# Attention and a Fourier mix on one core: the copy of attention sums goes to ScalarE, with an own order of products after each half, and the last reciprocal is taken on 16 columns

## The chip, the core and the metric

The kernel runs on one core of a Trainium2 chip. The core has five engines with queues of their own: TensorE (PE, its weight loads PEld), VectorE (DVE), ScalarE (ACT), GpSimd (POOL) and SyncE (SP), which here issues transfers only. TensorE writes into eight PSUM banks of 128 partitions x 512 fp32 values; VectorE and ScalarE read them out into SBUF. The metric is the device time of one execution in microseconds (us), the median of several.

## The reference

The input `x` has 2048 rows of 512. Two mixes of it are blended by a gate of each row:

```python
g = sigmoid((x * gate_w).sum(-1))                    # one number a row
q, k, v = split(x @ wqkv, heads=32, width=16)        # 32 heads
p = softmax((q @ k.T) * 16 ** -0.5)                  # 2048 x 2048 for each head
a = concat_heads(p @ v) @ wo
b = Re(DFT_seq(DFT_hidden(x)))                       # as products with cosines and sines
out = g * a + (1 - g) * b
```

## The kernel before

Heads are worked in 16 pairs (`NP`). A pair has two halves of 1024 queries, and a half has 16 steps, one for each block of 128 keys. Three kinds of product share TensorE; each uses 64 of its 128 rows, and products on the two row groups run side by side (the digit in a token is the row group):

- `e`, a score (line 725): keys x 512 queries into a PSUM bank. ScalarE takes the exponential out of it (line 707).
- `c`, a scan (line 758): scores of a later pair, of which VectorE takes only the maximum (line 760), since the softmax is shifted by it.
- `s`, a spectral product (line 983) of the Fourier part, summed over 48 products in the banks `z0` and `z1` and read out by VectorE (line 890, 892) when a group is complete.

Scores and scans share five banks, `b0` to `b4`. A planner, the class `Banks`, gives each of them the bank that is free soonest by its own model of when the engines get there; its constants (`period`, `release`, `late`) are times in ns. It moves nothing else: the order on TensorE is written out by hand.

From macro step `SINGLES` = 90 to `OUTM` = 234 the work stands in 72 blocks of two macro steps, that is, four steps of a half. The list `BLOCKS` says how many spectral products for each row group a block has: 24 in 48 of the blocks, 16 in 24 of them. `BLOCK_ORDERS` holds the order of the tokens of a block. All blocks of a size use one order. At the end of a block the value products of its four steps follow (`pv`, line 737): `e` times values, summed into one bank `pvb` over the 16 steps of a half. A column of ones beside the values gives the denominators of the softmax, one row of `pvb` in each of four quadrants.

After the 16th step `quotients` copies `pvb` to `ob` (line 770 or 772). GpSimd's queue sends the four denominator rows to a small tile `lc` (line 775); three macro steps later `divide` takes the reciprocal there, sends it to HBM and back, spread over partitions (`rb`), and multiplies on GpSimd (line 790). None of that is on TensorE. The next half's first value products come a block later, and overwrite `pvb`.

Four blocks make a half, so every fourth block follows a half end: 18 of the 72 blocks, 12 of size 24 and 6 of size 16.

The last half can't wait for transfers. Line 1184 copies it out in two halves of 256 columns; a product with a selection matrix `sel` (line 1188, built at the start in line 86) spreads the denominators over 128 partitions, VectorE takes reciprocals of 128 x 256 twice (lines 1200 and 1207) and multiplies, ScalarE and VectorE or GpSimd split the result into a high and a low part (`oh`, `ol`), and the last products of rows 8 to 15 (`part(t, 2)`, line 219) use these. "Row t" here is a block of 128 output rows. VectorE adds each product into its row (line 928), or ScalarE scales it and GpSimd adds (lines 1195 and 1196). The rows are then sent to HBM by SyncE's and ScalarE's queues (line 1220). Ten rows are still to be sent at this point.

Of the kernel before, what the change touches and what calls it, by code (L numbers as in the profile page):

```python
# [18 lines left out]
P = 128  # L19
# [36 lines left out]
}  # L56
BLOCK_SCANS = {24: 8, 16: 4}


def build(tc, x, xT, wqkv, wo, wrT, wiT, cr, ci, gate, out):  # L60
    nc = tc.nc
    with ExitStack() as ctx:
# [21 lines left out]
        sel = keep.tile([P, 4, 32], F32, name="sel")  # L84
        for n in range(4):
            nc.vector.tensor_copy(sel[:, n, :], ident[:, 32 * n + DH:32 * n + VC].to_broadcast([P, 32]))
        sel = sel.rearrange("p n m -> p (n m)")
# [546 lines left out]
        with ExitStack() as pa:  # L634
# [8 lines left out]
            def bank(tag, name="s"):  # L643
                return pools[0].tile([P, 512], F32, tag=tag, name=name)
# [18 lines left out]
            class Banks:  # L663

                slot, late, gap, load, group, weights, second = 226.0, 425.0, 93.0, 207.0, 854.0, 103.0, 56.0
# [101 lines left out]
            def quotients(p, h):  # L767
                ob = ap.tile([P, 512], F32, tag="ob", name="ob", bufs=2)
                if now[0] < OUTM - 1:
                    nc.vector.tensor_copy(ob, pvb)  # L770
                else:
                    nc.scalar.copy(ob, pvb)
                lc = sm.tile([P, 16], F32, tag="lc", name="lc")
                for n, (c, j, r) in enumerate(quads):
                    nc.gpsimd.dma_start(lc[32 * n:32 * n + 32, :],  # L775
                                        ob[r + DH:r + VC, :].rearrange("p (s e) -> p s e", e=16))
                return p, h, ob, lc
# [318 lines left out]
            for m in range(MACROS):  # L1096
# [46 lines left out]
                elif (m - SINGLES) % 2 == 0:  # L1143
                    size = BLOCKS[(m - SINGLES) // 2]
                    whole_block = BLOCK_ORDERS[size].split()
# [40 lines left out]
            spread = [bank("b0", "spread"), bank("b1", "spread")]  # L1186
            for c, ps in zip(halves_, spread):
                nc.tensor.matmul(ps[:, c], sel, ob[:, c], start=True, stop=True)
            part(3, 2)
            part(11, 0, 1)  # L1190

            def scaled(t, j):

                o = ap.tile([P, D], F32, tag="take", name="take", bufs=3)
                nc.scalar.mul(o, groups[t][j], g[:, t + 4 * j:t + 4 * j + 1])
                return lambda: nc.gpsimd.tensor_add(ys[t + 4 * j], ys[t + 4 * j], o)

            add = [scaled(3, j) for j in range(2)]
            c, ps = halves_[0], spread[0]
            nc.vector.reciprocal(rb[:, c], ps[:, c])  # L1200
            nc.vector.tensor_mul(ob[:, c], ob[:, c], rb[:, c])
            nc.scalar.copy(oh[:, c], ob[:, c])
            nc.gpsimd.tensor_sub(ol[:, c], ob[:, c], oh[:, c].bitcast(F32))
            for t in (8, 9):
                part(t, 2)
            c, ps = halves_[1], spread[1]
            nc.vector.reciprocal(rb[:, c], ps[:, c])
            nc.vector.tensor_mul(ob[:, c], ob[:, c], rb[:, c])
            nc.scalar.copy(oh[:, c], ob[:, c])
            nc.vector.tensor_sub(ol[:, c], ob[:, c], oh[:, c].bitcast(F32))  # L1210
            take_in(8, groups[8][0])
            for f in [scaled(8, 1)] + add:
                f()
            for t in (10, 11):
                part(t, 2)
# [31 lines left out]
```

## Time and profile before

| | us |
|---|---|
| median of three runs (1694.23 to 1701.38) | 1694.77 |
| the profiled execution's own time | 1694.55 |
| its span, first to last instruction | 1692.8 |
| first value product | 339.9 |
| value products of the first half end within the blocks, from | 716.95 |
| last value products of all | 1674.5 |

The profile's rows read: engine, line, operation, tile written <- tiles read; partitions x elements; then times. A group row gives the count, the busy time in us and the mean of one in ns, and after the bar the idle time before and what ended it. A row of a timeline starts with the start in us and the duration in us of neighbouring instructions that are merged, with their count behind `x`; in brackets stands the idle time ahead. A row of the chain in order of time has the start, the length and the count. VectorE and ScalarE overlap neighbouring instructions a little, so their starts are closer than their durations. A product of plain fp32 operands (the value products, the turn of the last half) appears as two loads and two products in the trace and as one in the order of instructions.

### The profile page before, as it was taken

To read this page: it belongs to the slowest core of one execution; us is meant where nothing else is said; L and a number is where in the kernel's file an instruction comes from. 1 tells how busy PE (TensorE), PEld (TensorE's weight loads), DVE (VectorE), ACT (ScalarE), POOL (GpSimd) and SP (SyncE) were. 2 spreads that over 40 slices of the span, in tenths; PEclk is the share of its full clock that TensorE was granted. 3 is DMA by queue.
4 is the path that set the end of the run, shared out by engine and by line. 5 is a ranking of instruction groups with operands and counts; after the bars stand their busy time and mean duration, and the time that the engine had idled before them with its cause. 6 is when DMAs were issued, how large, how long until landed. Compare 5 with 4: busy or idle time off the path is not lost.

```text
span 1692.8 us, 37028 instructions
## 1 busy us (share of the span) xinstructions
PE 1677.6 (99%) x13675; PEld 1074.6 (63%) x13675; DVE 1268.8 (75%) x2377; ACT 1291.3 (76%) x2410; POOL 706.6 (42%) x890
## 2 busy tenths in 40 slices
PE   9999999999999999999999999999999999999997
PEld 7877778833333333777776777566777777656554
DVE  5799899777777777888888888556888888656334
ACT  5689988799999999666665566777556665777885
POOL 1464301454662322364454444444535445445321
PEclk9999999999999999999999999999999999999999
DMA  8765234554542222243332332573332423335512
GB/s 281 234 231 154 68 121 145 176 187 126 144 128 70 61 70 74 64 115 95 92 100 82 101 97 86 149 245 87 118 107 80 127 90 113 104 108 151 160 40 100
DMA packets 140549, 206.61 MB, mean 122 GB/s; under 512 B 58880, under 2 KB 61936, under 8 KB 140368
## 3 DMA queue, kind: packets, MB, share of 16 engines
q1 hardware_dynamic: 98096, 173.76, 33.1%
q0 software_dynamic: 41696, 29.44, 6.7%
q8 instruction: 108, 1.77, 0.4%
q10 hardware_dynamic: 576, 1.05, 0.2%
q14 instruction: 73, 0.60, 0.1%
HBM read 137.89 MB, written 65.81 MB: 120 GB/s over the span
## 4 chain that ended last, share of the span: by engine, by line
PE 97%; DVE 1%; ACT 1%; issue 1%; POOL 0%; DVEq 0%; ACTq 0%; POOLq 0%
PE pvb L737 28%; PE z L983 24%; PE s L725 17%; PE s L758 9%; PE xy L350 6%; PE xy L371 6%; PE s L187 5%; PE s L364 0%; DVE y L928 0%; DVE fold L193 0%; DVE el L468 0%; ACT fold L191 0%; ACT eh L467 0%; PE s L611 0%; DVE rb L1200 0%
## 5 line engine op out<-in xcount | busy, mean ns | idle before, releaser
L707 ACT ACTIVATE e<-s 128x512 f32<-128x512 f32 (+1 forms) x1862 | 1014.4, 678 | 318.1 <-PE s L758 247.3
L760 DVE TENSOR_REDUCE mx<-s 128x1 f32<-128x512 f32 x1320 | 869.0, 688 | 233.3 <-PE s L758 167.3
L725 PE MATMUL s<-qs,ks 50*128 50x512 f32 x2040 | 620.1, 418 | 0.1
L983 PE MATMUL z<-b,chi 64*128 64x512 f32 x2060 | 513.9, 392 | 0.0
L737 PE MATMUL pvb<-e,va 128*17 128x512 f32 x4096 | 492.7, 595 | 0.3 <-DVE ob L770 0.3
L725 PEld LDWEIGHTS s<-qs,ks 50*128 50x128 f32 x2040 | 306.6, 185 | 212.0 <-ACT e L707 153.3
L758 PE MATMUL s<-ks,qs 48*128 48x512 f32 x1320 | 427.9, 402 | 0.0
L983 PE MATMUL z<-b,clo 64*128 64x512 f32 x1030 | 337.4, 394 | 0.0
L983 PEld LDWEIGHTS z<-b,chi 64*128 64x128 f32 x2060 | 324.8, 186 | 15.2
L193 DVE CUSTOM_DVE_ANT_0 fold<-s,fold 128x512 f32<-128x512 f32 x364 | 239.9, 689 | 24.6 <-ACT fold L191 7.4
L758 PEld LDWEIGHTS s<-ks,qs 48*128 48x128 f32 x1320 | 226.0, 185 | 34.5 <-issue 18.7
L737 PEld LDWEIGHTS pvb<-e,va 128*17 128x17 f32 x4096 | 92.2, 96 | 242.4 <-issue 237.3
L187 PE MATMUL s<-ks,qs 48*128 48x512 f32 x728 | 232.4, 400 | 1.6 <-ACT fold L191 1.2
L191 ACT ACTIVATE fold<-s 128x512 f32<-128x512 f32 x364 | 201.1, 605 | 28.0 <-PE s L187 26.9
L983 PEld LDWEIGHTS z<-b,clo 64*128 64x128 f32 x1030 | 173.5, 186 | 10.4 <-POOL clo L254 3.1
L775 POOL DMA_DIRECT2D lc<-ob x124 | 62.5, 510 | 249.9 <-DVE ob L770 214.1
L253 POOL CAST chi<-craw 128x512 fp32r<-128x512 f32 x126 | 77.3, 614 | 212.9 <-PE z L983 131.5
L254 POOL TENSOR_TENSOR clo<-craw,chi 128x512 fp32r<-128x512 f32 x126 | 161.8, 1284 | 10.4
L187 PEld LDWEIGHTS s<-ks,qs 48*128 48x128 f32 x728 | 132.6, 184 | 36.5 <-DVE mx L193 12.6
L371 PE MATMUL xy<-w,b 64*128 64x512 f32 x384 | 120.3, 399 | 0.0
L350 PE MATMUL xy<-w,b 64*128 64x512 f32 x384 | 117.0, 393 | 0.0
L928 DVE SCALAR_TENSOR_TENSOR y<-z,g,y 128x512 f32<-128x512 f32 x44 | 32.5, 750 | 75.2 <-PE z L983 69.7
(138 smaller groups left out, 1518.1 us busy)
## 6 DMA issues: line engine op xcount, KB each, us to landing
craw<-cr SPq DMA_DIRECT2D x64, 256.0 KB
craw<-ci SPq DMA_DIRECT2D x64, 256.0 KB
qs<-q_d SPq DMA_DIRECT2D x126, 128.0 KB
ks<-k_d SPq DMA_DIRECT2D x108, 128.0 KB
ab_d<-ab SPq DMA_DIRECT2D x32, 256.0 KB
y_d<-y SPq DMA_DIRECT2D x32, 256.0 KB
b<-bs_d SPq DMA_DIRECT2D x32, 256.0 KB
qs<-q_d SPq DMA_DIRECT2D x126, 64.0 KB
```

The costliest lines, as they stand in the source:

```text
L187: nc.tensor.matmul(ps, rows.q[qb // 8][b:b + 48, qb % 8 * P:(qb % 8 + 1) * P], rows.k[c // 2][b:b + 48, c % 2 * 512:(c % 2 + 1) * 512], st ...
L191: seen_by(nc.scalar.activation(fold[j], ps, AF.Relu))
L193: seen_by(nc.vector.tensor_tensor_reduce(out=fold[j], in0=ps, in1=fold[j], scale=1.0, scalar=-3.0e38, op0=ALU.add, op1=ALU.max, accum_out= ...
L254: sub(lo, raw, hi.bitcast(F32))
L350: ins = nc.tensor.matmul(ps, lhs[64:P], rhs[64:P], start=False, stop=last)
L371: nc.tensor.matmul(ps, lhs[0:64], rhs[0:64], start=n == 0, stop=False)
L707: nc.scalar.activation(e if j is None else e[:, j * 512:j * 512 + 512], ps, AF.Exp, scale=SCALE)
L725: nc.tensor.matmul(ps, rows.k[kb // 8][b:b + 50, kb % 8 * P:(kb % 8 + 1) * P], rows.q[h][b:b + 50, c * 512:c * 512 + 512], start=True, sto ...
L737: nc.tensor.matmul(pvb[r:r + VC, :], va[:, kb, 2 * p + j, :], es[step][c][0][:, j * 512:j * 512 + 512], start=kb == 0, stop=kb == NB - 1, ...
L758: nc.tensor.matmul(ps, rows.q[qb // 8][b:b + 48, qb % 8 * P:(qb % 8 + 1) * P], rows.k[c // 2][b:b + 48, c % 2 * 512:(c % 2 + 1) * 512], st ...
L760: nc.vector.tensor_reduce(mx[p][:, j, qb, c:c + 1], ps, axis=AX.X, op=ALU.max)
L983: nc.tensor.matmul(ps, pr_.lhs(j), pr_.rhs(j), start=group.count[j] == 1, stop=group.count[j] == group.size)
```

## The change

In the 18 half ends within the blocks ScalarE copies `pvb` instead of VectorE, as it did before in the last two; the copy is entered in `Banks` as 872 ns of ScalarE's time. The block behind a half end takes its tokens from a table of its own, `AFTER_HALF`, with the same numbers of `e`, `c` and `s`. In the last half, four products with four columns of the identity turn the denominators onto partitions (`den`, 128 x 16); the reciprocal is taken there, VectorE copies it out to 256 columns for each half of the columns (`inv4`), and four products with the identity turn it back, spread over 32 partitions each, into PSUM, from where VectorE multiplies with it. The two subtractions for `ol` are both on VectorE. GpSimd adds rows 3, 7, 12 and 13 instead of 3, 7 and 12, without being put back behind the turn. The transfers of the rows are dealt out anew, with rows 3 and 7 first.

```diff
+AFTER_HALF = {
...
+    16: "c0 e1 s0 s1 e0 c1 s0 s1 s0 e1 s0 s1 c0 s1 e0 s1 s0 s1 e0 c1 s0 s1 e0 s1 s0 c1 e0 s1 s0 s1 c0 e1 s0 s1 s0 e1 s1 c0 e1 s0 s1 s0 c1 e0 s1 s0 e1 s0 s1 e0 s0 e1 s0 s1 e0 e1",
+}
...
-        sel = keep.tile([P, 4, 32], F32, name="sel")
-        for n in range(4):
-            nc.vector.tensor_copy(sel[:, n, :], ident[:, 32 * n + DH:32 * n + VC].to_broadcast([P, 32]))
-        sel = sel.rearrange("p n m -> p (n m)")
...
-                slot, late, gap, load, group, weights, second = 226.0, 425.0, 93.0, 207.0, 854.0, 103.0, 56.0
+                slot, late, gap, load, group, weights, second, copy = 226.0, 425.0, 93.0, 207.0, 854.0, 103.0, 56.0, 872.0
...
                 ob = ap.tile([P, 512], F32, tag="ob", name="ob", bufs=2)
-                if now[0] < OUTM - 1:
+                if now[0] < SINGLES:
                     nc.vector.tensor_copy(ob, pvb)
                 else:
                     nc.scalar.copy(ob, pvb)
+                    banks.engine["e"] = max(banks.engine["e"], banks.t + banks.copy)
...
-                    whole_block = BLOCK_ORDERS[size].split()
+                    whole_block = (BLOCK_ORDERS if m % (NB // 2) else AFTER_HALF)[size].split()
...
-            spread = [bank("b0", "spread"), bank("b1", "spread")]
-            for c, ps in zip(halves_, spread):
-                nc.tensor.matmul(ps[:, c], sel, ob[:, c], start=True, stop=True)
-            part(3, 2)
-            part(11, 0, 1)
+            den = bank("b3", "den")
+            for b in range(4):
+                nc.tensor.matmul(den[:, 4 * b:4 * b + 4], ob[:, P * b:P * b + P], ident[:, DH:P:32], start=True, stop=True)
+            inv = sm.tile([P, 16], F32, name="inv")
+            nc.vector.reciprocal(inv, den[:, 0:16])
...
-                return lambda: nc.gpsimd.tensor_add(ys[t + 4 * j], ys[t + 4 * j], o)
...
+                nc.gpsimd.tensor_add(ys[t + 4 * j], ys[t + 4 * j], o)
+
+            part(3, 2)
+            for j in range(2):
+                scaled(3, j)
+            wide_ = ap.tile([P, 16, 32], F32, tag="ob", name="inv4", bufs=2)
+            spread = [bank("b0", "spread"), bank("b1", "spread")]
+            for h, c in enumerate(halves_):
+                nc.vector.tensor_copy(wide_[:, 8 * h:8 * h + 8], inv[:, 8 * h:8 * h + 8].to_broadcast([P, 8, 32]))
+                for b in (2 * h, 2 * h + 1):
+                    nc.tensor.matmul(spread[h][:, P * b:P * b + P], wide_[:, 4 * b:4 * b + 4].rearrange("p n k -> p (n k)"),
+                                     ident, start=True, stop=True)
+                part(11, h)
+                nc.vector.tensor_mul(ob[:, c], ob[:, c], spread[h][:, c])
+            for c in halves_:
+                nc.scalar.copy(oh[:, c], ob[:, c])
+                nc.vector.tensor_sub(ol[:, c], ob[:, c], oh[:, c].bitcast(F32))
+            for t in (8, 9, 10, 11):
                 part(t, 2)
-            for t, j in ((9, 0), (9, 1), (10, 0), (10, 1), (11, 0), (11, 1)):
-                take_in(t + 4 * j, groups[t][j])
-            for queue, rows in ((nc.sync, (8, 9, 3, 10, 7, 11)), (nc.scalar, (12, 13, 14, 15))):
+                take_in(t, groups[t][0])
+                if t < 10:
+                    scaled(t, 1)
+                else:
+                    take_in(t + 4, groups[t][1])
+            for queue, rows in ((nc.sync, (3, 7, 8, 12, 13)), (nc.scalar, (9, 10, 14, 11, 15))):
```

TensorE at the first half end within the blocks: the last value products (`pvb`) and what follows, before.

```order
L737 MATMUL pvb<-e,va 17x512 x16
L725 MATMUL s<-qs,ks 128x512
L758 MATMUL s<-ks,qs 128x512
L983 MATMUL z<-b_5729,chi 128x512
L725 MATMUL s<-qs,ks 128x512
L983 MATMUL z<-b_5730,chi 128x512
L983 MATMUL z<-b_5729,chi 128x512
L983 MATMUL z<-b_5729,clo 128x512
L758 MATMUL s<-ks,qs 128x512
L725 MATMUL s<-qs,ks 128x512
```

The same place now:

```order
L737 MATMUL pvb<-e,va 17x512 x16
L725 MATMUL s<-qs,ks 128x512
L758 MATMUL s<-ks,qs 128x512
L725 MATMUL s<-qs,ks 128x512
L758 MATMUL s<-ks,qs 128x512
L984 MATMUL z<-b_5724,chi 128x512
L725 MATMUL s<-qs,ks 128x512
L984 MATMUL z<-b_5725,chi 128x512
L984 MATMUL z<-b_5724,chi 128x512
L984 MATMUL z<-b_5724,clo 128x512
```

A second score and a second scan have moved ahead of the first spectral product (`z`), which gives ScalarE and VectorE two pieces each in the first four products.

ScalarE from the last blocks to its end, before; `e` are exponentials, `take` rows scaled for GpSimd, `chi` high parts.

```order
L707 ACTIVATE e<-s 128x512 x1210
L772 COPY ob<-pvb 128x512
L707 ACTIVATE e<-s 128x512 x64
L772 COPY ob<-pvb 128x512
L707 ACTIVATE e<-s 128x512 x56
L1195 ACTIVATE take<-s_24958,g 128x512
L1195 ACTIVATE take<-s_24959,g 128x512
L1202 CAST chi<-ob 128x256
L1209 CAST chi<-ob 128x256
L1195 ACTIVATE take<-s_25004,g 128x512
```

Now the copies stand among the exponentials; the start of what was one stretch of 1210:

```order
L707 ACTIVATE e<-s 128x512 x50
L772 COPY ob<-pvb 128x512
L707 ACTIVATE e<-s 128x512 x64
L772 COPY ob<-pvb 128x512
L707 ACTIVATE e<-s 128x512 x64
```

Every 64 exponentials, which are one half, a copy of the sums has come in; it is behind all exponentials of the half and ahead of those of the next.

VectorE in the last half, from the copy of the sums to the first row (`y`), before.

```order
L1184 COPY ob<-pvb 128x256 x2
L1200 RECIPROCAL rb<-spread 128x256
L1201 TENSOR_TENSOR ob<-ob,rb 128x256
L1207 RECIPROCAL rb<-spread 128x256
L1208 TENSOR_TENSOR ob<-ob,rb 128x256
L1210 TENSOR_TENSOR clo<-ob,chi 128x256
L928 SCALAR_TENSOR_TENSOR y_23635<-s_25003,g,y_23635 128x512
```

And now:

```order
L1185 COPY ob<-pvb 128x256 x2
L1191 RECIPROCAL inv<-den 128x16
L1205 COPY inv_24986<-inv 128x256
L1210 TENSOR_TENSOR ob<-ob,spread 128x256
L1205 COPY inv_24986<-inv 128x256
L1210 TENSOR_TENSOR ob<-ob,spread 128x256
L1213 TENSOR_TENSOR clo<-ob,chi 128x256 x2
L929 SCALAR_TENSOR_TENSOR y_23630<-s_25014,g,y_23630 128x512
```

One reciprocal of 16 columns stands where two of 256 stood, two copies out to 256 columns have come in, each ahead of products on TensorE that its multiplication waits for, and both subtractions now stand ahead of the first row.

More of the change, by code (lines that the diff above doesn't have):

```diff
@@ L56 @@
 }
+AFTER_HALF = {
+    24: "e0 c1 e0 c1 s0 e1 s0 s1 s0 s1 s1 s0 s1 c0 e1 s0 s1 s0 c1 s0 s1 e0 e1 s0 s1 c0 s1 s0 s1 s0 e0 c1 e0 s1 s0 s1 c0 s1 s0 e1 s1 s0 c1 s0 s1 e0 s1 s0 e1 c0 s1 s0 s0 e1 s0 c1 e0 s1 s0 s1 c0 e1 s0 s1 s0 e1 s0 c1 c0 s1 s0 s1 e0 s1 s0 s1 c0 s1 c0 c1",
+    16: "c0 e1 s0 s1 e0 c1 s0 s1 s0 e1 s0 s1 c0 s1 e0 s1 s0 s1 e0 c1 s0 s1 e0 s1 s0 c1 e0 s1 s0 s1 c0 e1 s0 s1 s0 e1 s1 c0 e1 s0 s1 s0 c1 e0 s1 s0 e1 s0 s1 e0 s0 e1 s0 s1 e0 e1",
+}
 BLOCK_SCANS = {24: 8, 16: 4}
@@ L1195, in scaled @@
                 nc.scalar.mul(o, groups[t][j], g[:, t + 4 * j:t + 4 * j + 1])
[L1196 to L1203, printed above, removed]
@@ L1204, in build @@
-            for t in (8, 9):
-                part(t, 2)
[L1206 to L1215, printed above, removed]
```

## The prediction

> **What bounds the kernel.** I read the page first (busy times, then the chain), next the chain stretch by stretch, next the timelines of VectorE, ScalarE and TensorE at one half end, and last the timeline of the final 20 us.
>
> ```profile
> PE 1677.6 (99%) x13675; PEld 1074.6 (63%) x13675; DVE 1268.8 (75%) x2377; ACT 1291.3 (76%) x2410; POOL 706.6 (42%) x890
> PE 97%; DVE 1%; ACT 1%; issue 1%; POOL 0%; DVEq 0%; ACTq 0%; POOLq 0%
> ```
>
> TensorE sets the time: 97% of the chain is its own. What another engine does counts only where TensorE waits for a PSUM bank, and behind TensorE's last product. The page cannot show such a wait, since a product that starts late still reads as busy. The chain in order of time can: each block of products ends in one run of value products (`pvb`), so the distance of two runs is the length of a block. A half ends in the run at 716.95 (blocks of 24) and in the run at 1509.94 (blocks of 16).
>
> ```profile
> 716.95 3.56 PE pvb L737 x32
> 730.37 3.56 PE pvb L737 x32
> 743.55 3.56 PE pvb L737 x32
> ...
> 1509.94 3.56 PE pvb L737 x32
> 1520.45 3.56 PE pvb L737 x32
> 1530.72 3.56 PE pvb L737 x32
> ```
>
> A block of 24 after a half end lasts 730.37 - 716.95 = 13.42 us, the next one 13.18. A block of 16 after a half end lasts 10.51 us, the next one 10.27. So a half end costs 0.24 us in either kind. There are 72 blocks, four to a half: 18 half ends, 12 before blocks of 24 and 6 before blocks of 16.
>
> **What the 0.24 us are.** The copy of the sums stands ahead of the scans on VectorE:
>
> ```profile
> L770 DVE COPY ob<-pvb x29: 690/692/694, 369.6 to 1555.1; 128x512 f32<-128x512 f32 x29
> ...
> 720.64 0.69 DVE L770 COPY ob<-pvb 128x512 f32<-128x512 f32 x1 [1.73 <-PE pvb L737]
> 721.25 4.69 DVE L760 TENSOR_REDUCE mx<-s 128x1 f32<-128x512 f32 x7
> ...
> 734.42 4.97 DVE L760 TENSOR_REDUCE mx<-s 128x1 f32<-128x512 f32 x7 [0.47 <-PE s L758]
> ...
> 720.44 0.50 PE L725 MATMUL s<-qs,ks 50*128 50x512 f32 x1
> 733.86 0.49 PE L725 MATMUL s<-qs,ks 50*128 50x512 f32 x1
> ```
>
> After a half end the first scan is read 721.25 - 720.44 = 0.81 us after the block's first product; in the next block 734.42 - 733.86 = 0.56. VectorE starts 0.25 us late, reads scans back to back, and TensorE, which has five banks for scores and scans together, loses about the same 0.24 us later in the block.
>
> **Part 1: the copy on ScalarE.** It leaves VectorE at these 18 half ends (the 11 earlier ones of the 29 stay). The last two half ends already do it this way:
>
> ```profile
> L772 ACT COPY ob<-pvb x2: 586/586/587, 1599.3 to 1639.9; 128x512 f32<-128x512 f32 x2
> ...
> 1639.76 0.50 PE L983 MATMUL z<-b,b 64*128 64x512 f32 x1
> ...
> 1639.94 0.59 ACT L772 COPY ob<-pvb 128x512 f32<-128x512 f32 x1 [0.49 <-issue]
> 1640.42 3.13 ACT L707 ACTIVATE e<-s 128x512 f32<-128x512 f32 x6
> ...
> 734.45 6.16 ACT L707 ACTIVATE e<-s 128x512 f32<-128x512 f32 x12 [4.79 <-PE s L758]
> 1524.57 8.01 ACT L707 ACTIVATE e<-s 128x512 f32<-128x512 f32 x16 [2.28 <-PE s L725]
> ```
>
> The copy itself is hidden: ScalarE stands idle for 4.79 us (2.28 in a block of 16) while the value products run, and nothing is queued ahead of the copy. Behind it wait the exponentials of the new block. The first can start 1640.42 - 1639.76 = 0.66 us after the block's first product; without a copy it starts 734.45 - 733.86 = 0.59 us after. So ScalarE is put back by 0.07 us where VectorE was put back by 0.25. If this cover were gone (a copy that starts late), up to 0.59 us would stand before the first exponential, and in a block of 16 ScalarE has no pause to make it up: there 16 exponentials run back to back for 8.01 us of 10.27. The GpSimd DMAs that wait for the copy get their sums 0.1 us sooner and stand on no path.
>
> **Part 2: the own order after a half end.** It has as many products of each kind, so TensorE's own work is the same; only waits can differ. In a block of 24 it feeds two scores and two scans before the first spectral product, where the old one feeds one of each: ScalarE and VectorE both have a second piece of work sooner. No trace shows this order. Bounds: at best no wait is left and a block costs what its neighbours cost, 18 x 0.24 = 4.3 us gained; at the other end one wait as large as the old one stays, 0 gained. Passing on the whole 0.07 us would take back 1.3. I take 0.03 us lost in each, near the good end since 0.07 is the largest delay that a row gives: 18 x (0.24 - 0.03) = 3.8 us gained.
>
> **Part 3: the last half.** From here on the chain leaves TensorE:
>
> ```profile
> 1675.07 1.23 PEld L219 LDWEIGHTS s<-b,b 64*128 64x128 f32 x12 [0.85 <-issue]
> 1675.30 0.76 DVE L1184 COPY ob<-pvb 128x256 f32<-128x256 f32 x2 [2.50 <-PE pvb L737]
> 1676.66 0.73 PEld L1188 LDWEIGHTS spread<-ob,sel 128*128 128x128 f32 x4 [0.36 <-issue]
> 1677.45 1.76 DVE L1200 RECIPROCAL rb<-spread 128x256 f32<-128x256 f32 x1 [1.39 <-issue]
> 1678.72 1.27 ACT L1195 ACTIVATE take<-s,g 128x512 f32<-128x512 f32 x2 [5.67 <-PE s L219]
> 1681.38 0.43 DVE L1208 TENSOR_TENSOR ob<-ob,rb 128x256 f32<-128x256 f32 x1
> 1682.62 4.03 DVE L928 SCALAR_TENSOR_TENSOR y<-s,g,y 128x512 f32<-128x512 f32 x6
> 1682.91 3.73 POOL L1196 TENSOR_TENSOR y<-y,take 128x512 f32<-128x512 f32 x3 [1.81 <-ACT take L1195]
> ...
> L782 DVE RECIPROCAL lc<-lc 128x16 f32<-128x16 f32 x31 | 7.6, 244 | 0.0
> GB/s 0 0 0 312 382 304 0 0 0 31 0 0 0 0 0 0 0 0 0 0 0 0 0 269 379 382 382 375 367 394 390 367 383 382 378 390 156 0 0 0
> ```
>
> The last row cuts 1672 to 1693 into 40 slices of 0.525 us. From the first finished row on the writes run at about 382 GB/s without a hole until 1691: ten rows of 262 KB at 0.69 us are 6.9 us, longer than VectorE's seven remaining sums (to 1687.3). So the end is the first row's time plus the queue of rows. The change touches both.
>
> The queue: rows 3 and 7 no longer wait behind the turn; they leave before row 8. Eight rows remain, 2 x 0.69 = 1.4 us less. Rows 12 and 13 need 0.68 us on ScalarE and 1.27 on GpSimd behind row 8's products, and come before the queue reaches them.
>
> The first row: now VectorE starts row 8 at 1682.62. New steps from 1676.66, when the array is free: 8 passes for `den` (four products, two passes each, as the two of L1188 gave four loads). A load costs between (1.23 - 0.18) / 11 = 0.095 (half-height weights) and, nearest in shape, (0.73 - 0.19) / 3 = 0.18 us; I take 0.18: done at 1678.2 with 0.25 us through the array. Reciprocal of 16 columns 0.24 (two of 1.76 go). Copy out to 256 columns about 0.42: 1678.9. Four passes and the way back to VectorE 0.95: 1679.8. Product 0.43: 1680.2. Then the second half's copy, its passes (0.95), its product (0.43), one subtraction (0.43) and the third product of row 8 (0.3): with nothing in the way row 8 starts at 1682.7, no gain from the shorter reciprocals, because the way over TensorE is walked twice in a row.
>
> But something is in the way. GpSimd now adds row 3 from about 1679.8 on (the passes of `part(3, 2)` follow `den`, ScalarE needs 0.68), and beside a GpSimd operation VectorE's SBUF-to-SBUF work is held:
>
> ```profile
> L211 DVE CAST chi<-mt x16: 172/181/1229, 110.3 to 1563.2; 128x32 fp32r<-128x32 f32 x16
> ...
> 1562.66 1.28 POOL L840 TENSOR_TENSOR b<-wor,b 128x512 fp32r<-128x512 f32 x1
> 1563.21 1.23 DVE L211 CAST chi<-mt 128x32 fp32r<-128x32 f32 x1
> ```
>
> A cast of 0.18 us took 1.23 when it met a GpSimd sum. The second copy of the turn, due at 1680.2, meets row 3's sum (to 1681.1) and waits 0.9 us: row 8 starts at 1683.6, 1.0 later than now. The sums of rows read PSUM and go on beside GpSimd (the 4.03 us beside the 3.73). Together -1.4 + 1.0 = -0.4 us. Ends: no meeting (-1.4 + 0.1) and loads at 0.095 (16 passes, 1.4 sooner), -2.7; both GpSimd sums ahead of the copy, another 1.27, +0.9. I take -0.4.
>
> A rule that would spoil this part: the Trainium skill (FP8 and Floating Point Precision, TensorE Precision Notes) says that a true FP32 product takes four passes through the array. By it the turn has 16 more passes than I counted. The rows show two loads for each call, against it.
>
> **Part 4: the four copies for `sel` go.** They stand before 2.4 us, while TensorE waits for its first loads: nothing.
>
> **Sum.** 1692.8 of span - 3.8 - 0.4 = 1688.6, against a profiled run of 1694.55 with its start and end: 1690.35. The median of the runs shown is 0.22 above that run: 1694.77 - 4.2 = **1690.6 us**.
>
> **Rivals.** *A, the wait only moves.* The new order leaves one wait per block, for a bank of an exponential instead of a scan: blocks gain 0, 1694.4. For it: five banks serve both engines and no row has the order. Against: the delay is 0.07 instead of 0.25.
> *B, slower.* ScalarE's copy comes late or its exponentials queue behind it for the whole 0.59 us, and blocks of both sizes lose that where they lost 0.24: 18 x 0.35 = 6.3 - 0.4, giving 1700.7. It decides once a half end loses more than 0.26 us. For it: the 8.01 us without a pause. Against: the 0.66 us seen at 1639.76.
> *C, four passes in the turn.* 16 more at 0.18 put row 8 back 2.9 us: 1693.5. Against: four loads for two products.
> *D, the turn is held twice by GpSimd,* or not at all: 1691.9 or 1689.7, within my own case.
>
> **Chances.** Forecast with D 0.74 (1687.8 to 1692.5), A 0.16, B 0.06, C 0.04. The range runs from the good ends of both parts, 4.3 in the blocks and 2.7 in the tail, to A: 1687.8 to 1694.4. A difference of 0.5% (8.5 us) is about what a measurement can tell from none. Faster by more needs twice all waits that the chain shows: 0.02. Slower by more is the far side of B (0.71 us lost at each half end): 0.03. Within: 0.95.
>
> **What would show it.** In the chain, runs after half ends at 13.2 and 10.3 us (A: 13.4 and 10.5 as now; B: 13.8 and 10.9). VectorE's copy of the sums x11, ScalarE's x20 at 586 ns, the exponential behind it 0.66 us after the block's first product. In the end, row 8's sum near 1683.6 less the blocks' gain, a copy to 256 columns longer than 0.42 us beside GpSimd, eight loads for `den`. The forecast is wrong if a block in the middle of a half changes its length, since nothing there was meant to move.

## The result, and the profile after

The changed kernel takes 1688.09 us in the median of nine runs (1687.93 to 1689.18), the kernel before 1694.55 beside it (1694.07 to 1701.38). The ratio is 0.9959, with an interval from 0.9949 to 0.9969. Forecast were 1690.6 us: the direction and the range held, the gain was 6.5 us instead of 4.2. In several kernels a few executions take 3 to 7 us longer than the others (1701.38 here; four of twelve in the run below with the old tile of `sel` not filled, whose median they raise by 0.6), and since the ratios weigh every execution, they are not exactly those of the medians.

The page of the changed kernel, busy times and chain:

```profile
PE 1672.5 (99%) x13687; PEld 1070.8 (63%) x13687; DVE 1255.2 (74%) x2356; ACT 1302.3 (77%) x2429; POOL 707.5 (42%) x890
PE 96%; issue 1%; ACT 1%; DVE 1%; POOL 0%; DMA 0%; SPq 0%; DVEq 0%; ACTq 0%; POOLq 0%
```

TensorE is still the bound. VectorE lost 13.6 us of work and ScalarE got 11; neither is what the time shows. The chain in order of time, at the same two half ends that the prediction read, and at a third:

```profile
715.48 3.56 PE pvb L737 x32
728.59 3.56 PE pvb L737 x32
741.77 3.56 PE pvb L737 x32
...
1075.24 3.56 PE pvb L737 x32
1086.02 3.56 PE pvb L737 x32
...
1504.21 3.56 PE pvb L737 x32
1514.51 3.56 PE pvb L737 x32
1524.78 3.56 PE pvb L737 x32
```

A block of 24 behind a half end lasts 728.59 - 715.48 = 13.11 us, less than its neighbour's 13.18. A block of 16 there lasts 10.30, as forecast; but the one that begins behind 1075.24 takes 10.78, more than the 10.5 of before. Summed over all runs of value products in the traces (each stretch ends where the last of its value products begins):

| us | ahead of the blocks | 72 blocks | between | behind the last value products | span |
|---|---|---|---|---|---|
| before | 680.37 | 882.66 | 111.52 | 18.22 | 1692.77 |
| changed | 678.89 | 878.08 | 111.29 | 18.37 | 1686.63 |
| difference | -1.48 | -4.58 | -0.23 | +0.15 | -6.14 |

The 12 blocks of 24 behind a half end went from 161.37 us together to 157.20 (-0.35 each), the 6 of 16 from 61.41 to 61.16: four gained 0.15 to 0.22 each, two lost 0.25 and 0.27. The other 54 blocks moved by 0.1 us in all; the largest move of one of them is 0.19 (a block of 16, from 10.50 to 10.31).

The copies of the sums, by line, and ScalarE, VectorE and TensorE at the half end behind 715.48:

```profile
L770 DVE COPY ob<-pvb x11: 691/692/692, 368.4 to 672.5; 128x512 f32<-128x512 f32 x11
L772 ACT COPY ob<-pvb x20: 585/587/588, 719.1 to 1633.7; 128x512 f32<-128x512 f32 x20
...
718.97 0.50 PE L725 MATMUL s<-qs,ks 50*128 50x512 f32 x1
719.15 0.59 ACT L772 COPY ob<-pvb 128x512 f32<-128x512 f32 x1 [4.37 <-PE pvb L737]
719.54 10.78 DVE L760 TENSOR_REDUCE mx<-s 128x1 f32<-128x512 f32 x16 [2.10 <-PE s L758]
719.63 2.10 ACT L707 ACTIVATE e<-s 128x512 f32<-128x512 f32 x4
```

The first exponential comes 719.63 - 718.97 = 0.66 us behind the block's first product, the first scan is read at 0.57 (0.81 before). Both are what Part 1 said.

The end of the changed kernel: VectorE, the loads of the turn, GpSimd, the queues, and what was moved in 40 slices of 0.5 us from 1667 on.

```profile
1668.78 1.23 PEld L219 LDWEIGHTS s<-b,b 64*128 64x128 f32 x12 [0.85 <-issue]
1670.37 0.97 PEld L1189 LDWEIGHTS den<-ident,ob 128*128 128x128 f32 x8 [0.36 <-issue]
1671.46 0.26 DVE L1191 RECIPROCAL inv<-den 128x16 f32<-128x16 f32 x1 [1.70 <-PE den L1189]
1671.82 0.29 DVE L1205 COPY inv<-inv 128x256 f32<-128x256 f32 x1
1673.12 2.56 POOL L1197 TENSOR_TENSOR y<-y,take 128x512 f32<-128x512 f32 x2 [25.58 <-ACT take L1196]
1673.34 1.21 DVE L1205 COPY inv<-inv 128x256 f32<-128x256 f32 x1
1674.60 0.52 PEld L1207 LDWEIGHTS spread<-ident,inv 128*128 128x128 f32 x4 [1.18 <-DVE inv L1205]
1675.69 0.98 DVE L1213 TENSOR_TENSOR clo<-ob,chi 128x256 fp32r<-128x256 f32 x2
1676.93 3.43 DVE L929 SCALAR_TENSOR_TENSOR y<-s,g,y 128x512 f32<-128x512 f32 x5 [0.26 <-PE s L219]
1678.39 4.78 ACTq L1223 DMA_DIRECT2D out_dram<-y  x5
...
GB/s 94 385 385 184 0 0 0 33 0 0 0 0 0 0 0 0 172 352 0 352 172 0 0 340 176 57 377 164 377 389 381 385 389 369 377 393 37 0 0 0
```

From the first product behind the last value products to row 8's sum it is 1676.93 - 1668.78 = 8.15 us, and was 1682.62 - 1675.07 = 7.55 before: 0.6 later. The second copy out took 1.21 us beside GpSimd's sum, the first 0.29: held for 0.92, as forecast. The row of GB/s is the surprise: where the writes ran without a hole before, they now come in pieces from 1675 on and run densely only from about 1681.

### The profile page after: what moved, and what is told of

Same layout as the page of the kernel before. It is cut to its first block, busy times and chain, and to the rows that moved or that the text cites. A ratio compares the mean times of both kernels' runs of the same rounds, so it can differ in the third digit from the quotient of the medians.

```text
span 1686.6 us, 37096 instructions
## 1 busy us (share of the span) xinstructions
PE 1672.5 (99%) x13687; PEld 1070.8 (63%) x13687; DVE 1255.2 (74%) x2356; ACT 1302.3 (77%) x2429; POOL 707.5 (42%) x890
## 4 chain that ended last, share of the span: by engine, by line
PE 96%; issue 1%; ACT 1%; DVE 1%; POOL 0%; DMA 0%; SPq 0%; DVEq 0%; ACTq 0%; POOLq 0%
PE pvb L737 28%; PE z L984 24%; PE s L725 17%; PE s L758 10%; PE xy L371 6%; PE xy L350 6%; PE s L187 5%; PE s L364 0%; PE s L219 0%; POOL xg L561 0%; DMA qs<-q_d 0%; DVE el L468 0%; DVE y L929 0%; ACT eh L467 0%; ACT fold L191 0%
```

## The experiments

Ahead of them stands the theory that these rows led to. In a block of 16 the 0.24 us of a half end are VectorE's, as the prediction had it. In a block of 24 they are not. The loads of TensorE in the kernel before, in the first block of 24 of the prediction, then GpSimd there, and then who waited for GpSimd's low part of the coefficients (`clo`, line 254) in the whole kernel, us and times:

```profile
725.68 0.18 PEld L983 LDWEIGHTS z<-b,clo 64*128 64x128 f32 x1 [0.24 <-POOL clo L254]
...
721.62 2.01 POOL L775 DMA_DIRECT2D lc<-ob  x4 [7.87 <-DVE ob L770]
723.63 0.62 POOL L253 CAST chi<-craw 128x512 fp32r<-128x512 f32 x1
724.34 1.29 POOL L254 TENSOR_TENSOR clo<-craw,chi 128x512 fp32r<-128x512 f32 x1
...
  PEld z L983: 3.1, 12
```

Behind the copy of the sums GpSimd issues four DMAs for the denominators (2.01 us); the split of the next spectral coefficients is queued behind them and ends at 725.63. A spectral product waits for it 0.24 us here and 0.24 to 0.27 in all, 12 times, once in each of the 12 blocks. In a block of 16 the load of a scan is what waits, for VectorE:

```profile
1515.05 0.18 PEld L758 LDWEIGHTS s<-ks,qs 48*128 48x128 f32 x1 [0.40 <-DVE mx L760]
```

So the rival to the prediction's one cause: in blocks of 24 it is when the new coefficients are first asked for, which the order of the tokens sets.

**The start alone.** The changed kernel with `sel` built again.

```diff
+        sel = keep.tile([P, 4, 32], F32, name="sel")
+        for n in range(4):
+            nc.vector.tensor_copy(sel[:, n, :], ident[:, 32 * n + DH:32 * n + VC].to_broadcast([P, 32]))
...
```

> The changed kernel with the four copies for sel built at the start again (unused). Between the two traces the first value product came 1.2 us sooner. If the start of the changed kernel is faster because sel is gone, the first value product is back at 339.9 us and the time near 1689.3. If the difference is scatter of the first loads, the first value product lies anywhere within half a us of 338.8 to 339.9 and the time stays near 1688.1.

1689.02 us, ratio to before 0.9971 (0.9953 to 0.9989). The blocks are as in the changed kernel (878.05), the stretch ahead of them ends at 679.59 instead of 678.89. The first value product comes at 339.17, neither at the 339.9 of the kernel before nor at the 338.77 of the changed one; by itself that decides nothing. More on this below.

**Every product with its own coefficients.** The kernel before, with one change. `state["c"]` is replaced when the first row group begins a unit; a row group that lags takes the last product of the old unit with the next unit's tile. Here each product keeps the tile of its own unit.

```diff
-                                state["c"] = parts.pop(0)
+                                state["c", s // CS] = parts.pop(0)
...
-                        yield Product(group, lambda j, i=i, w=w: state["c"][i // 2][64 * j:64 * j + 64, w, :],
+                        yield Product(group, lambda j, s=s, i=i, w=w: state["c", s // CS][i // 2][64 * j:64 * j + 64, w, :],
```

TensorE's order there, before and with the edit; Pool_49 is the wait for GpSimd, and the first `b` belongs to the old unit:

```diff
 L983 MATMUL z<-b_5850,chi 128x512
 L725 MATMUL s<-qs,ks 128x512 [waits Activation_49]
-L983 MATMUL z<-b_5849,clo 128x512 [waits Pool_49]
+L983 MATMUL z<-b_5849,clo 128x512
 L758 MATMUL s<-ks,qs 128x512 [waits DVE_49]
 L983 MATMUL z<-b_5893,chi 128x512
 L983 MATMUL z<-b_5894,chi 128x512
 L725 MATMUL s<-qs,ks 128x512 [waits Activation_49]
-L983 MATMUL z<-b_5893,clo 128x512 x2
+L983 MATMUL z<-b_5893,clo 128x512 [waits Pool_49]
+L983 MATMUL z<-b_5893,clo 128x512
```

> The kernel before, with one change: every spectral product reads the coefficients of its own unit of 12. In the kernel before, the row group that lags takes its last products of a unit from the unit that the other group has just opened, so TensorE needs the new unit's low part (clo), which GpSimd still makes, three products sooner. Theory of the prediction (VectorE's late scans fill the banks): nothing changes, blocks after a half end 13.45 and 10.51 us, time 1694.5. Second theory (in blocks of 24 TensorE waits for GpSimd's clo, which stands behind the four transfers lc): 13.2 after a half end in blocks of 24, 10.51 in blocks of 16, 12 x 0.25 = 3.0 us less, 1691.5.

1690.76 us, 0.9978 (0.9970 to 0.9987). Nothing waits for `clo` any more, and the chain at the same place reads:

```profile
716.28 3.56 PE pvb L737 x32
729.48 3.56 PE pvb L737 x32
742.67 3.56 PE pvb L737 x32
```

The block behind the half end lasts 13.20 us, its neighbour 13.19; the blocks of 16 stay at 10.51 to 10.54. VectorE's copy and its late scans are all still there (the first is read 0.82 us behind the block's first product). So in blocks of 24 the copy on VectorE cost TensorE nothing through the scans; the whole 0.24 us was the wait for GpSimd.

**The copy alone**, and **the order alone**, each put into the kernel before.

```diff
...
-                if now[0] < OUTM - 1:
+                if now[0] < SINGLES:
                     nc.vector.tensor_copy(ob, pvb)
                 else:
                     nc.scalar.copy(ob, pvb)
+                    banks.engine["e"] = max(banks.engine["e"], banks.t + banks.copy)
```

> The kernel before, with the copy of the sums on ScalarE in the 18 half ends and the planner's entry for it, with the old order everywhere and the old end. Theory of the prediction: the delay of VectorE is gone, 13.2 and 10.3 us after a half end, 1690.2. Second theory: blocks of 16 go to 10.3; in blocks of 24 GpSimd's transfers and so clo come only 0.13 us sooner, 13.30 after a half end; 12 x 0.13 + 6 x 0.2 = 2.8 us less, 1691.7.

```diff
...
-                    whole_block = BLOCK_ORDERS[size].split()
+                    whole_block = (BLOCK_ORDERS if m % (NB // 2) else AFTER_HALF)[size].split()
```

> The kernel before, with the own order after half ends, the copy still on VectorE, the old end. Theory of the prediction: VectorE's first scan is as late as before, blocks after a half end no shorter than 13.45 and 10.51, time 1694.5 or more. Second theory: in blocks of 24 the first product that needs the new clo stands later (token 46 instead of 43), 13.2 or a little more by the scans, while two blocks of 16 (those in which a spectral group begins) need it sooner (token 41 instead of 44) and rise to 10.9: about 2.3 us less, 1692.2.

The copy alone: 1691.7 us, 0.9988 (0.9979 to 0.9997). The order alone: 1690.6 us, 0.9979 (0.9970 to 0.9988), 1.6 less than its second theory: 1.2 of that is that the 12 blocks of 24 came out at 13.10 and not at 13.2. By blocks behind a half end, summed from the traces (the last block of 16 is shorter, since it has fewer scans, and is left out of the column of single blocks):

| us | 12 blocks of 24 | one of them | 6 blocks of 16 | one of them |
|---|---|---|---|---|
| before | 161.37 | 13.42 to 13.47 | 61.41 | 10.51 to 10.55 |
| copy alone | 160.24 | 13.29 to 13.35, one 13.62 | 60.29 | 10.30 to 10.37 |
| order alone | 157.15 | 13.07 to 13.12 | 62.26 | 10.52 to 10.94 |
| changed: both | 157.20 | 13.08 to 13.12 | 61.16 | 10.30 to 10.82 |

In the block of 13.62 the load of a score waits 0.31 us for an exponential of ScalarE, besides the wait for `clo`. In blocks of 24 the order does it all. In the old one row group 0 opens the next unit at token 38 (counted from 0), while row group 1 writes the last product of the old unit at token 43, with the new `clo`. In the new order both groups are through with the old unit before either opens the next, and the first product that needs the new `clo` stands at token 46. The copy on ScalarE is done 0.1 us sooner and GpSimd with it, which is worth 0.12. In blocks of 16 the copy does it: the six waits of 0.40 for VectorE go with it and stay without it. With the copy alone, though, the load of a scan in each of the six waits 0.19 for an exponential of ScalarE; in the changed kernel, with both, none does. Who waited for VectorE's scans (line 760), first before, then with the copy alone:

```profile
  PEld s L758: 4.5, 9
```

```profile
  PEld s L758: 2.1, 3
```

The order of 16 makes two blocks worse, since row group 1 opens the unit at token 40 and the lagging group 0 asks for the new `clo` at 41; in the old order that is token 44. These are the two where a spectral group begins right behind the half end:

```profile
1079.86 2.02 POOL L776 DMA_DIRECT2D lc<-ob  x4 [2.78 <-ACT ob L772]
1081.87 0.63 POOL L253 CAST chi<-craw 128x512 fp32r<-128x512 f32 x1
1082.59 1.28 POOL L254 TENSOR_TENSOR clo<-craw,chi 128x512 fp32r<-128x512 f32 x1
...
1083.92 0.18 PEld L984 LDWEIGHTS z<-b,clo 64*128 64x128 f32 x1 [0.47 <-POOL clo L254]
```

This is the changed kernel, GpSimd and then the load that waits.

**The changed kernel again, and two tokens swapped.** In the second kernel the last product of the lagging row group comes ahead of the token with which the other group opens the next unit, so it takes its own unit's tile.

```diff
-    16: "... s0 s1 c0 e1 s0 s1 s0 e1 s1 c0 e1 s0 s1 s0 c1 e0 ..."
+    16: "... s0 s1 c0 e1 s0 s1 s0 e1 s1 c0 e1 s0 s0 s1 c1 e0 ..."
```

> The changed kernel as it is, beside the three that follow. 1.5 us of its gain lie ahead of the blocks, where nothing that was changed shows a cost. If that part is scatter of the first loads between two executions, the end of the value products ahead of the blocks falls into the span of the kernels with sel (679.5 to 680.4 us) and the gain over the kernel before is near 5 us by the median; if it belongs to the change, it stays near 678.9 and the gain near 6.3.

> The changed kernel, with two neighbouring tokens of the order for 16 exchanged (40 and 41), so that row group 0 takes its last product of a unit before row group 1 opens the next. Second theory: the first product that needs the new clo moves from token 41 to 48, and the two blocks in which a group begins fall from 10.8 to 10.3 us: 1.0 us less than the changed kernel. If these two blocks wait for a PSUM bank instead, they stay at 10.8.

The changed kernel again: 1688.65 us, 0.9973 (0.9959 to 0.9986). With the swap: 1687.08, 0.9958 (0.9945 to 0.9970). The chain of the second at the half end where the changed kernel needed 10.78:

```profile
1074.50 3.56 PE pvb L737 x32
1084.82 3.56 PE pvb L737 x32
```

That is 10.32 us, and all five full blocks of 16 behind a half end now last 10.30 to 10.32. Nothing waits for `clo` anywhere. The blocks together are 1.06 us shorter than in the changed kernel's second profile (876.85 against 877.91), two waits of 0.47 and a little.

The stretch ahead of the blocks of the changed kernel ends at 678.77 this time, near the 678.89 of its first profile, as by the theory that the start belongs to the change. Its gain over the kernel before beside it (1694.08) is 5.4 us by the medians, nearer to the other theory.

**The turn's copies first.** Both copies out to 256 columns are done before the first product of the turn, so that none of them meets GpSimd's row 3.

```diff
-            for h, c in enumerate(halves_):
+            for h in range(2):
                 nc.vector.tensor_copy(wide_[:, 8 * h:8 * h + 8], inv[:, 8 * h:8 * h + 8].to_broadcast([P, 8, 32]))
+            for h, c in enumerate(halves_):
                 for b in (2 * h, 2 * h + 1):
```

> The changed kernel, with both copies out to 256 columns made in the last half before the first multiplication, so before GpSimd starts to add row 3. If the second copy (1.21 us instead of 0.29) is held by GpSimd's sum, it takes 0.3 now, row 8 starts 0.9 us sooner and the stretch from the last value product to the end falls from 18.4 to about 17.5 us. If the end is set by how the rows are dealt out to the queues, it falls by less than 0.4.

1687.84 us, 0.9963 (0.9950 to 0.9975). The stretch from the last value product to the end fell from 18.37 to 18.03 us, not to the 17.5 of the first theory. VectorE in its turn, with the marks of the changed kernel's rows:

```profile
1668.85 1.23 PEld L219 LDWEIGHTS s<-b,b 64*128 64x128 f32 x12 [0.85 <-issue]
...
1671.90 0.49 DVE L1205 COPY inv<-inv 128x256 f32<-128x256 f32 x2
1674.94 1.40 DVE L1214 TENSOR_TENSOR clo<-ob,chi 128x256 fp32r<-128x256 f32 x2
1676.60 3.46 DVE L929 SCALAR_TENSOR_TENSOR y<-s,g,y 128x512 f32<-128x512 f32 x5 [0.25 <-PE s L219]
```

The copies are no longer held (0.49 for both), and row 8 comes 1676.60 - 1668.85 = 7.75 us behind the mark instead of 8.15. That is less than the 0.92 that the copy had been held: the two subtractions, 0.98 us in the changed kernel, now meet GpSimd's second sum (row 7, to 1675.7) and take 1.40. The hold went to the next instruction that could be held. The Trainium skill (SBUF — State Buffer, Who interferes with whom) says that a VectorE instruction with two inputs in SBUF contends with a GpSimd instruction that reads SBUF, and that with at most one such input, outside the modes in which it uses both ports, it doesn't. The 1.40 of the subtractions against 0.98 and the sums of rows (one input in PSUM), which go on at 0.69 each beside GpSimd, agree.

**All three.** The swap, the copies first, and the new order of 24 in all 48 blocks of 24 instead of 12.

```diff
...
-                    whole_block = (BLOCK_ORDERS if m % (NB // 2) else AFTER_HALF)[size].split()
+                    whole_block = (BLOCK_ORDERS if m % (NB // 2) and size == 16 else AFTER_HALF)[size].split()
...
```

> The changed kernel with the exchange of e6, the copies of e7, and the order for 24 that was used after half ends in all blocks of 24. After half ends a block of 24 takes 13.10 us, elsewhere 13.17 by the old order. If that is the order's doing, the 36 other blocks gain 0.07 each, 2.6 us, and the whole is 2.6 + 1.0 + 0.9 = 4.5 us below the changed kernel. If it belongs to the place after a half end, only 1.9 us.

1683.55 us (1682.95 to 1684.80), 0.9938 (0.9926 to 0.9951), faster than both kernels, and 5.1 us below the changed kernel beside it, where 4.5 were expected. The other 36 blocks of 24 went from 474.2 to 471.5 us, 13.10 each: the new order is better even where no copy stands ahead of it. Why is not shown. In the new order of 24, two neighbouring tokens share a row group in four places and in the old one in nine, but in the orders of 16 it is two against six, and there the new order gains nothing over a block of the old in the middle of a half (10.31 against 10.31). The end became 0.94 us shorter than in the run before (17.09 against 18.03), with the same code behind the last value products and row 8 at the same 7.75 us. Where that came from is seen in ScalarE's queue, which issues five of the last ten rows. The issues of the changed kernel, shortest, median and longest in ns, and then, of the queues that moved bytes from 1678.4 to 1680.4, the one that brings instructions (transfers, MB, share):

```profile
L1223 ACTq DMA_DIRECT2D out_dram<-y x5: 410/602/2020, 1678.4 to 1682.6; - x5
...
q14 instruction: 1, 0.01, 2.1%
```

And the issues of the version with all three:

```profile
L1224 ACTq DMA_DIRECT2D out_dram<-y x5: 338/379/813, 1674.4 to 1677.0; - x5
```

In the changed kernel the first of ScalarE's five issues (row 9) takes 2.02 us, and the other four rows queue behind it; in that time, an instruction load of queue 14 runs. In the version with all three the issue takes 0.38, and the last load of that queue ran some 30 us earlier. The seven profiles whose last load of queue 14 falls on that issue have it at 1.84 to 2.22 us; the three where it does not (the two runs with all three and the one below with rows on VectorE) have none over 0.95. That queue 14 brings ScalarE's instructions is inferred from this; which kernel has the load where was not steered.

**What `sel` is at the start: its place, or its copies.** The changed kernel, once with the old tile allocated and not filled, once with the four copies made into the tile of ones.

```diff
+        sel = keep.tile([P, 4, 32], F32, name="sel")
+        nc.gpsimd.memset(sel[:, 0, 0:1], 0.0)
```

> The changed kernel with the tile of the old sel (512 bytes of each partition) allocated again at its old place, and one column of it set to zero on GpSimd, but without the four copies on VectorE. The end of the value products ahead of the blocks (five profiles with the copies and the tile: 679.5 to 680.4 us; five without both: 678.3 to 679.2) tells the theories apart. Theory S, the place of everything behind the tile in the memory of the cores counts: 679.4 to 680.4, and a run about 0.9 us longer than the changed kernel. Theory C, the four copies count, because they put the first work of VectorE back by 1.45 us: 678.3 to 679.2, and no change of the run. Theory N, both groups are one scatter that happened to part: anywhere from 678.3 to 680.4. I hold C a little likelier than N, and S least likely.

```diff
+        for n in range(4):
+            nc.vector.tensor_copy(ones, ident[:, 32 * n + DH:32 * n + VC].to_broadcast([P, 32]))
         nc.vector.memset(ones, 1.0)
```

> The changed kernel with the four small copies on VectorE again, into the tile of ones (which is set to one behind them), so no tile is added. Theory C (the copies count): the value products ahead of the blocks end at 679.4 to 680.4 us, and the run is about 0.9 us longer than the changed kernel. Theory S (the place of the tiles counts): 678.3 to 679.2 and no change. Theory N (one scatter): anywhere from 678.3 to 680.4.

1689.07 us, 0.9977 (0.9965 to 0.9990), and 1688.66, 0.9963 (0.9950 to 0.9976): by time neither differs from the changed kernel. The stretch ahead of the blocks ends at 679.13 and at 679.06, inside the group without `sel`, so at this place theory C failed for the copies (679.4 to 680.4) and S for the tile. The seven profiles without it reach from 678.31 to 679.42, the five with it from 679.49 to 680.37; the means are 1.0 us apart.

The copies are a part of that 1.0. From the first value product to the end of the stretch it takes 340.42 to 340.48 us in the six profiles with the four copies (the five with `sel`, and the copies into the tile of ones), and 340.04 to 340.13 in the eight without them, the one with the place of `sel` among these. The 0.35 us come in one step, at the half end near 612 us: in the six, the copy of the sums begins 0.38 to 0.40 us after VectorE's last work, and in the eight at most 0.04 after it. The copy and the value products that wait for it, in the kernel before:

```profile
613.31 0.69 DVE L770 COPY ob<-pvb 128x512 f32<-128x512 f32 x1 [0.38 <-PE s L725]
614.05 0.13 PEld L737 LDWEIGHTS pvb<-e,va 128*17 128x17 f32 x8 [0.76 <-DVE ob L770]
```

And in the changed kernel:

```profile
611.83 0.69 DVE L770 COPY ob<-pvb 128x512 f32<-128x512 f32 x1
612.58 0.13 PEld L737 LDWEIGHTS pvb<-e,va 128*17 128x17 f32 x8 [0.42 <-DVE ob L770]
```

Why four copies at 1.3 us make another one late at 613 these rows don't tell. The rest of the 1.0 lies ahead of the first value product, which comes at 338.57 to 339.93 with the copies and at 338.26 to 339.32 without: there the groups overlap, and it may be chance.

**Rows 3 and 7 on VectorE**, in its two pauses of the turn, on top of all three; and **all three once more**.

```diff
-            for j in range(2):
-                scaled(3, j)
...
                 part(11, h)
+                take_in(3 + 4 * h, groups[3][h])
                 nc.vector.tensor_mul(ob[:, c], ob[:, c], spread[h][:, c])
```

> The best version so far (both orders in all blocks, both copies of the turn ahead of its first product), with rows 3 and 7 taken in by VectorE in its two pauses of the turn (0.68 and 1.11 us long, while the passes of spread run), instead of a product on ScalarE and a sum on GpSimd. Nothing of GpSimd then runs beside the turn. If GpSimd is what holds VectorE there, as I say, the two subtractions take 0.86 us together (1.40 now), and the third product of row 8 comes 0.3 to 0.6 us sooner after the last value product than in the run of the same code with rows 3 and 7 on GpSimd, less what the two sums (0.69 each) stand out over the pauses: 0 to 0.3. Time: 0 to 0.6 us shorter than that run. If the 1.40 belongs to the subtractions themselves (two operands in SBUF), they stay at 1.40, and the two sums make the turn up to 0.3 us longer.

> The best version so far once more, beside the three others of this call: the time again 4 to 6 us below the changed kernel, and 10 to 11.5 us below the kernel before. Its end behind the last value product was 17.1 us, where the same code of the turn with the other orders had 18.0; if that 0.9 is a matter of when the last rows land, it comes out between 17.0 and 18.2 here, with row 8's sum at the same distance from the last value product as there.

1683.07 us, 0.9931 (0.9917 to 0.9944), and 1683.11, 0.9930 (0.9915 to 0.9945). VectorE at the end of the first:

```profile
1666.12 1.23 PEld L219 LDWEIGHTS s<-b,b 64*128 64x128 f32 x12 [0.85 <-issue]
...
1669.69 0.75 DVE L929 SCALAR_TENSOR_TENSOR y<-s,g,y 128x512 f32<-128x512 f32 x1
1670.69 0.74 DVE L929 SCALAR_TENSOR_TENSOR y<-s,g,y 128x512 f32<-128x512 f32 x1
1672.21 0.98 DVE L1213 TENSOR_TENSOR clo<-ob,chi 128x256 fp32r<-128x256 f32 x2
1673.46 3.43 DVE L929 SCALAR_TENSOR_TENSOR y<-s,g,y 128x512 f32<-128x512 f32 x5 [0.27 <-PE s L219]
```

With nothing of GpSimd beside them the subtractions are back at 0.98, and row 8 stands 1673.46 - 1666.12 = 7.34 us behind the mark, 0.41 sooner than in the same code with GpSimd. The end is 16.63 us against 17.06. In the time of a run these 0.4 us do not show: in the profiles the stretch ahead of the blocks was 0.76 and the blocks 0.66 us longer than in the other, in code that is the same. The repetition of all three has its end at 17.06 us, against 17.09, and none of ScalarE's issues over 0.81: the short end belongs to that kernel and not to one execution.

## Why the prediction was right or wrong

**The bound and the size of a half end** stand: 0.24 us, 18 times, on TensorE.

**The step that failed** is the one from the late scans to the lost time, and with it the sum. The prediction had one cause for all 18 half ends, VectorE's scans, put back by the copy. In 12 of them the cost was another wait: a spectral product waited 0.24 to 0.27 us for GpSimd's `clo`. In the sum, the shorter queue of Part 3 and the "nothing" of Part 4 were wrong as well. The prediction also took a difference under 0.5% for one that can hardly be told from none; the interval of 0.9949 to 0.9969 tells this one.

**What the 0.24 us are** failed for 12 of the 18. "VectorE starts 0.25 us late ... and TensorE ... loses about the same 0.24 us later in the block" holds in blocks of 16, where the load of a scan waits for VectorE 0.40 us and the copy alone gives back 0.19 (61.41 to 60.29 in six). In blocks of 24 the scans cost nothing: with the copy still on VectorE and only the coefficients' tile changed, the block lasts 13.20. The two equal numbers, 0.24 and 0.24, suggested one cause; there were two.

**Part 1** was right in its rows (copies x20 at 587 ns, x11 on VectorE, the exponential at 0.66), and wrong in one sentence: that the GpSimd DMAs behind the copy "stand on no path". In the blocks of 24 they were the path: behind them GpSimd splits the coefficients for which TensorE waited.

**Part 2** had its reason wrong and its size near: 3.8 us forecast, 4.58 measured in all 72 blocks. In blocks of 24 the gain does not come from a second score and scan ahead of the spectral products but from asking later for the new `clo`. That the size came near is luck: a cost that was measured right was given to a cause that it did not have, and the change happened to remove the true one too. The good end that the prediction set, a block as long as its neighbours, was no bound: the old order is itself 0.07 us longer in every block of 24 than the new one (13.17 against 13.10), as the run with all three showed. On the other side, two blocks of 16 lost 0.25 and 0.27 us: there the wait moved, as rival A had it, though to GpSimd and not to an exponential.

**Part 3**: -0.4 forecast, +0.15 measured. Of its terms, the hold of the second copy was right (0.9 forecast, 0.92 measured). The eight loads of `den` were right in number and cost 0.97 us, 0.12 each, not 0.18: row 8 came 0.6 us later, not 1.0. The term that failed is the shorter queue: "eight rows remain, 2 x 0.69 = 1.4 us less" assumes writes without a hole, and ScalarE's half of the rows stood behind an issue of 2.02 us. Taking out the 0.95 us by which the end differs with and without that issue gives 18.37 - 0.95 = 17.42, 0.8 below before, which is 0.6 - 1.4; this is worked out, since no run has the changed kernel's own end without the load.

**Part 4**, "nothing", was wrong in part: the stretch ahead of the blocks was 1.48 us shorter. Of that, 0.32 lie behind the first value product, and there the four copies cost some 0.35 in all six profiles that have them. The other 1.16 lie ahead of it (339.93 against 338.77) and stay open: over all profiles that place moves by more than this, and the groups with and without the copies overlap there.

**The sum.** The gain forecast in the span was 3.8 + 0.4 = 4.2; 6.14 were found: 4.58 in the blocks, 1.48 ahead of them, 0.23 between them and the end, less 0.15 at the end. So the 1.9 us that were missed are 0.8 in the blocks, 0.2 behind them and the 1.5 ahead of them that were not expected at all, less the 0.55 by which the end came out worse.

**The rivals.** A did not happen in 16 of the 18 blocks; in the other two the wait moved, to GpSimd. Half of the change would have come near it: with the copy alone, the six blocks of 16 had a wait of 0.19 for an exponential. B did not: the exponential's 0.66 held. C did not: `den` has eight loads for its four products, two for each, as the prediction counted against the rule of the Trainium skill (FP8 and Floating Point Precision, TensorE Precision Notes) of four passes; by the number of loads the trace is against it. D is in Part 3: the turn was held once, by 0.92.

**The own test** of the forecast, that no block in the middle of a half changes, held for their sum: 54 blocks, 0.1 us, one of them 0.19 shorter. It would have told nothing of the wrong cause. What the loads of TensorE wait for, block by block, would have.

## What to carry to other kernels

Equal losses in two places are not yet one cause: ask at each place which load of TensorE waits, and for whom, before a copy is moved. When several row groups work through units of data at different paces, look at which token first asks for the next unit; here the order alone gained 3.7 us and the copy alone 2.6, by the medians. A transfer queue that is counted as dense has to be checked issue by issue, on each engine that issues.

## What the runs showed that was not expected

An issue of a transfer on ScalarE took 1.84 to 2.22 us instead of 0.38 where an instruction load of queue 14 fell on it, in seven profiles of seven, and between two kernels with the same code at the end that made 0.95 us. These two differ only in the order of tokens, hundreds of us earlier.

The hold of VectorE by GpSimd was passed on when one operation was freed from it: the copy took 1.21 us and the subtractions 0.98; with both copies moved ahead, these took 0.49 together and the subtractions 1.40.

Eight plain fp32 loads of 128 x 128 in a row took 0.97 us, 0.12 each, where the four of the old turn had suggested 0.18.

Four small copies on VectorE in the first 2 us went with a copy of the sums that began 0.38 us late at 613 us, in six profiles of six, and with 0.35 us more of TensorE's time; without them none of eight had it.
